# Four edits to a planned transformer kernel: a closing GpSimd addition, the norm's root in four tasks, a repriced exp, and filler chosen unit by unit

## The chip, the cores and the metric

The kernel runs on one core of one Trainium2 chip. The metric is the device time of one execution in microseconds (us), median over runs; lower is better. Engine names in the profile: PE (TensorE matmuls) and PEld (its weight loads), DVE (VectorE), ACT (ScalarE), POOL (GpSimd), SP (SyncE, which only issues transfers here).

## The reference, cut to what matters

Two layers share one set of weights. Each layer is an attention block with 32 heads of 16 features, then a dense block with a ReLU, each behind a layer norm and added to x. x has 2048 rows of 512 features; the dense block is 1792 wide.

```python
scores = jnp.einsum("bhqd,bhkd->bhqk", q, k) * (Dh ** -0.5)
p = _softmax(scores, axis=-1)
o = jnp.einsum("bhqk,bhkd->bhqd", p, v)
...
x = x + _A_ref(_layernorm(x, axis=-1), A_wqkv, A_wo)
x = x + _B_ref(_layernorm(x, axis=-1), B_w1, B_w2)
x = x + _A_ref(_layernorm(x, axis=-1), A_wqkv, A_wo)
x = x + _B_ref(_layernorm(x, axis=-1), B_w1, B_w2)
```

The softmax needs the exponential of 2 x 32 x 2048 x 2048 scores. The kernel cuts them into units of 128 keys by 512 queries of one head, 4096 units in all (later chunks with fewer queries put several blocks into a unit).

## The kernel before, in words

**Slots.** The main loop (`while units`) goes in slots. A slot takes three units: PE computes their scores into one of two PSUM tiles `ps_s` (L1714), and ACT takes the exponential of that tile into a buffer `e` in one instruction (L1727). There are 1366 slots.

**Integer pairs.** ACT need not do all units. In most slots the third unit is left out of ACT's instruction and goes to DVE, which adds a bias and makes a 16-bit integer `lin` out of it (L1299), whose bits read as bf16 are a coarse exponential. Two such units make a pair. GpSimd makes two shifted copies of a pair, `up` and `down`, with 64-bit integer additions (L1354), and PE sums values against all three versions, so that the errors cancel. A pair therefore saves ACT two units of 512 columns and costs DVE two instructions, GpSimd two, and PE three value products in place of one for each unit. Whether a slot starts a pair is decided from the plan's clocks: free buffers, the backlog of DVE (`now_dve[0] + waiting < now_pe[0] + BACKLOG`, 3000 ns), GpSimd's queue, and `press()`, the pressure of dated filler.

**Value rounds and filler.** Between the score matmuls PE does value products (L1175, into `ps_o`, four heads at once in a round) and filler: projections, the dense block, transposes (L564, L645, into `ps_f`). Every filler group ends in a DVE instruction that takes its sums out of PSUM (L745, L781, L835, L874, L914 and others).

**The plan.** All instructions are put in order on the host while the program is built, by a planner that keeps a clock for PE, DVE, GpSimd and SP and a price for each step: a matmul unit is `MM` = 216 ns, a DVE evacuation 612 ns, an exp `1280.0 * place[m] / (W * QS) + 63.3` ns (1280 for 1536 columns). `exp_end[no]` is when the plan expects slot `no`'s exp to end. From it comes `limit`, up to which PE may be filled before the next scores. `fill_pe(limit)` does filler while the account `owed` is above zero (each slot adds `pace`, what is left over what remains of the chunk). `fill_v(limit, least)` does value rounds, each with at least `least` of the four column groups ready (3 before). A slot calls them as filler, rounds, filler, or, when at least four slots' exps are pending, as rounds, filler, rounds. If PE then still has time in the plan, the scores are computed again up to that time (`times`), which keeps the PE clock up. DVE's tasks wait in `dve_q` and are taken by `run_dve` in order of rank and place; `musts`, the integer pairs' first steps and the copies of `ps_o`, go ahead of them. An engine runs its instructions in the order written, so the order of the plan is what the chip does, whenever operands are ready.

**The layer norm.** `ln_stats` (L600) per row block of 128, then `ln_root`: aggregation (L606), variance plus epsilon (L607), a seed of the reciprocal root by integer arithmetic (L611), a cubic step and a Newton step (L622 to L628), then `ln_apply` (L636), which makes `xn`; SP transposes `xn` by transfer, or PE does. The plan has the root as one task of `RSTD` = 1600 ns, put at the head of DVE's queue (`place=0`). There are 13 roots of four row blocks, 3 of two, 2 of one.

**The head.** Ahead of the loop the first norm is written out by hand: GpSimd builds the identity (masks.py:199, an affine-select), DVE reduces it to masks (L1387), takes statistics of the first four row blocks (L600), and GpSimd takes the root by a power (L1413). Then `xn` (L1425), transposes (L645), K and Q of the first heads (L1443), the first scores. ACT interleaves the first weight columns (`wkq`, L213), GpSimd the others, and loads two of the weight blocks itself (`load_w(nc.gpsimd, k, 1)`, L209). A trial INT64_ADD (L1474) follows. Constants such as `X_AT` and `WQ_AT` tell the plan when loads are there; the plan's clock starts with `exp_end = {-1: 11350.0, 0: 12350.0}`.

**The tail.** After the last scores, the last chunk's output projection, norm and dense block run on PE, DVE and ACT; GpSimd has nothing left.

Of the kernel before, what the change touches and what calls it, by code (L numbers as in the profile page):

```python
# [13 lines left out]
I32 = mybir.dt.int32  # L14
# [4 lines left out]
ALU = mybir.AluOpType  # L19

EPS = 1e-5
GAIN = 64.0 / 9.0
RSQRT_SEED = 0x5F3759DF
# [3 lines left out]
def kernel(  # L27
# [10 lines left out]
    nc = tc.nc  # L38
# [13 lines left out]
    QS = 512  # L52
# [5 lines left out]
    W = 3  # L58
# [33 lines left out]
    LOADED, FIRST_LOAD = 18000.0, 30  # L92
    BOTH = 4
    WHOLE = 4
    STARTS, MORE, LEAST, SLIP = {}, {}, {}, {}
    X_AT = (8.3, 8.5, 9.5, 10.6, 11.0, 11.4, 11.8, 12.1, 12.5, 12.8, 13.3, 14.0)
    WQ_AT, WV_AT = {0: 0.0, 1: 10600.0, 2: 16000.0, 3: 17400.0}, 10200.0
    FIRST_TRANSPOSE = 1600.0
    VLAG = 1
    RSTD = 1600.0  # L100
    Q_SPARE = 6
    V_LATE, CALM = 3, 1.2
    AHEAD = (8.0, 8.0)
# [77 lines left out]
    stats = [sb([P, TPC, nc.vector.BN_STATS_DIM], FP32, f"stats{n}") for n in range(2)]  # L181
    mv = [sb([P, TPC, nc.vector.BN_AGGR_DIM], FP32, f"mv{n}") for n in range(2)]
    va2 = sb([P, 2, TPC], FP32, "va")
    va_ = [va2[:, n] for n in range(2)]
    ya2 = sb([P, 2, TPC], FP32, "ya")
    ya_ = [ya2[:, n] for n in range(2)]
# [110 lines left out]
    two = [True]  # L297
# [98 lines left out]
    def do_piece():  # L396
        c, fn, ready, kind = cur.popleft()
        pe_run(kind, c, ready)
        fn()
        owed[0] -= c  # L400
# [9 lines left out]
            worst = max(worst, units_due / max(when - slot[0] - 1, 0.5))  # L410
        return worst

    def fill_pe(limit):

        while owed[0] > 0:
            limit_now = limit if owed[0] < 5.0 or not hurry[0] else now_pe[0] + 1000.0
            if not cur:
                if len(evac) > two[0]:
                    return
                free = bank_free[next_bank()] + DVE_TO_PE  # L420
                start = pe_start("f", free) + 50.0
                for g in urgent + sorted(work, key=lambda g: g.get("waits", False)):
                    t = at(g["deps"], "pe")
                    if t is not None and t <= start:
                        break
                else:
                    return
                if pe_start(g["kind"], free) + 50.0 + g["pieces"][0][0] * MM > limit_now:
                    return
                start_group(g)  # L430
            elif pe_start(cur[0][3], cur[0][2]) + cur[0][0] * MM > limit_now:
                return
            do_piece()

    def do_task(t):
        if t["engine"] == "pool":
            pool_q.remove(t)
            now_pool[0] = max(now_pool[0], at(t["deps"], "pool")) + t["cost"]
        else:
            dve_q.remove(t)  # L440
            dve_run(t["cost"], at(t["deps"], "dve"))
        t["fn"]()
        for k in t["makes"]:
            if k not in made:
                mark(k, t["engine"])
# [148 lines left out]
    def ln_n(tag):  # L594
        return ln_seq.index(tag) % 2
# [3 lines left out]
            ln_seq.append(tag)  # L599
        nc.vector.bn_stats(out=stats[ln_n(tag)][:, i, :], in_=x_t[tt][:])  # L600

    def ln_seed(tag, rows, gain):

        n = ln_n(tag)
        for i in range(rows):
            nc.vector.bn_aggr(out=mv[n][:, i, :], in_=stats[n][:, i, :])  # L606
        nc.vector.tensor_scalar(  # L607
            out=va_[n][:, 0:rows], in0=mv[n][:, 0:rows, 1], scalar1=EPS, scalar2=gain,
            op0=ALU.add, op1=ALU.mult,
        )  # L610
        nc.vector.tensor_scalar(  # L611
            out=ya_[n][:, 0:rows].bitcast(I32), in0=va_[n][:, 0:rows].bitcast(I32), scalar1=-0.5,
            scalar2=float(RSQRT_SEED), op0=ALU.mult, op1=ALU.add,
        )

    def ln_root(tag, rows):

        n = ln_n(tag)
        ln_seed(tag, rows, GAIN)
        a, y, t1 = va_[n][:, 0:rows], ya_[n][:, 0:rows], ta_[n][:, 0:rows]  # L620
        stt = nc.vector.scalar_tensor_tensor
        nc.vector.tensor_mul(out=t1, in0=y, in1=y)  # L622
        nc.vector.tensor_mul(out=t1, in0=t1, in1=a)
        stt(out=t1, in0=t1, scalar=-10.0 / 3.0, in1=t1, op0=ALU.add, op1=ALU.mult)
        stt(out=y, in0=t1, scalar=5.0, in1=y, op0=ALU.add, op1=ALU.mult)
        stt(out=t1, in0=y, scalar=-0.5 / GAIN, in1=y, op0=ALU.mult, op1=ALU.mult)
        nc.vector.tensor_mul(out=t1, in0=t1, in1=a)
        stt(out=y, in0=t1, scalar=1.5, in1=y, op0=ALU.add, op1=ALU.mult)  # L628

    xn_waits = [0]  # L630
    xn_free = [0.0]
# [27 lines left out]
    def ln_rows(tag, tt, n, i):  # L659

        if tag not in ln_seq:
            ln_seq.append(tag)
        at_tag = ln_seq.index(tag)
        prev = ln_seq[at_tag - 1]
        rows_of_prev = chunks[prev[1:]][1]
        before_that = ln_seq[at_tag - 2] if at_tag > 1 else None
        old = each(chunks[before_that[1:]][1], "xn", before_that) if at_tag > 1 else []
        if ("st", tag, i) not in made:
            loaded = [("x", tt + i)] * (tag[0] == "ln1" and not tag[1])
            task(720, lambda: ln_stats(tag, tt + i, i), [("st", tag, i)], old + loaded)  # L670
        if i == n - 1:

            task(
                RSTD, lambda: ln_root(tag, n), [("rs", tag, 3)], each(n, "st", tag) + old, place=0
            )

            def apply(k):
                ln_apply(tag, tt + k, k)
                if not by_dma(tag):
                    return  # L680
                _, l, j = tag
                xn_waits[0] -= k == TPC - 1
                nc.sync.dma_start_transpose(
                    out=xnT[j][:, :, k * P : (k + 1) * P], in_=xnbuf[k][:]
                )
                sp_free[0] = max(sp_free[0], now_dve[0] + 200.0) + first_transpose[0]
                first_transpose[0] = 0.0
# [50 lines left out]
    def each(n, *key):  # L738
        return [key + (i,) for i in range(n)]
# [237 lines left out]
    segs = []  # L977
# [38 lines left out]
    sums_wait = [0]  # L1016
# [150 lines left out]
    pend = deque()  # L1167
# [15 lines left out]
    seg_at = [0]  # L1183
# [55 lines left out]
            finish_segment(sg, sg is segs[-1])  # L1239
            seg_at[0] += 1  # L1240

    def fill_v(limit, least):

        done = 0
        while not sums_wait[0] and seg_at[0] < len(segs):
            if two[0] and (len(pend) < BOTH or cur or evac):
                break
            t = v_start()
            if t + MM > limit:
                break  # L1250
            sg = segs[seg_at[0]]
            found = v_ready(sg, t)
            if len({f[1][2] for f in found}) < min(least, sum(r > 0 for r in sg["rem"])):
                break
            v_round(found, t)
            done += 1
        return done
# [126 lines left out]
    tag = ("ln1", 0, 0)  # L1384
    idle_matmuls(13)
    for e in range(2):
        nc.vector.tensor_reduce(  # L1387
            out=mask[e],
# [4 lines left out]
            out=qmask[:, e : e + 1],  # L1393
# [5 lines left out]
            op0=ALU.mult,  # L1399
# [166 lines left out]
    while units:  # L1566
# [121 lines left out]
        need_by = exp_end[no - 1] - MM - PE_TO_ACT  # L1688
        limit = max(need_by - 60.0, s_ready) - SWITCH + SLIP.get(no, 0.0)
        late = len(pend) >= 4  # L1690
        for kind in ("v", "f", "v") if late else ("f", "v", "f"):
            if kind == "f":
                fill_pe(limit)
            else:
                fill_v(limit, LEAST.get(no, 3))

        spare = int(max(need_by - pe_start("s", s_ready), 0.0) / MM)
        soon = (len(pend) > 1) + (owed[0] > 1.0 and (bool(cur) or not evac and any(
# [33 lines left out]
            if a >= place[m]:  # L1732
                tc.declare_no_dep(ex.ins, score, reason="different PSUM banks")
        begin = max(exp_end[no - 1], now_pe[0] + PE_TO_ACT)
        exp_end[no] = begin + 1280.0 * place[m] / (W * QS) + 63.3
        for reader, banks in readers[no % 2]:
            if W - 1 in banks and len(banks) == 1:
                tc.declare_no_dep(
# [36 lines left out]
    while True:  # L1775
        t = next(
            (t for t in dve_q + pool_q if at(t["deps"], t["engine"]) is not None), None
        )
        if t is None:
            break  # L1780
        do_task(t)
    users.clear()
    l, j = 1, LAST
    tag = ("ln2", l, j)
# [169 lines left out]
```

## Time and profile before

| | us |
|---|---|
| Median of 3 runs | 1454.89 (1453.84 to 1458.4) |
| The profiled execution | 1457.04 |
| Its span, first to last instruction | 1455.3 |
| ACT busy | 1388.2 (95%) |
| PE busy | 1367.2 (94%) |
| DVE busy | 1137.0 (78%) |
| POOL busy | 711.3 (49%) |
| Mean granted PE clock | 0.987 |

The profile is of one execution. The busy time of an engine is the union of its instructions' times, so on ACT, where one exp starts before the last has drained, it hides short waits. "Idle before" counts gaps ahead of an instruction, and what is named behind it is what ended the wait; "issue" is a wait for nothing that the profile shows. The chain of waits goes back from the last instruction to whatever released each step. Some matmul records can be missing.

### The profile page before, as it was taken

How to read it: one execution, taken by the hardware profiler on the slowest of the kernel's cores; microseconds unless marked ns; L12 is line 12 of the kernel's file. 1: busy time of each engine (PE TensorE's matmuls, PEld its weight loads, DVE VectorE, ACT ScalarE, POOL GpSimd, SP SyncE). 2: the span in 40 equal slices, each digit the busy share in tenths (PEclk: the TensorE clock that was granted, in tenths of full speed). 3: DMA queues.
4: the chain of work that ended last, by engine and by line, in shares of the span. 5: the costliest groups of instructions: out<-in, count | busy, mean ns of one | idle time of the engine just before them, and what ended most of it. 6: DMA issues, size and time to landing. Idle time of an engine off the chain costs nothing.

```text
span 1455.3 us, 49098 instructions
## 1 busy us (share of the span) xinstructions
PE 1367.2 (94%) x20895; PEld 497.9 (34%) x20898; DVE 1137.0 (78%) x2078; ACT 1388.2 (95%) x1392; POOL 711.3 (49%) x1203
## 2 busy tenths in 40 slices
PE   6899889999999999999899999989999999999997
PEld 2322222222232222222222222223234444455665
DVE  5777668877887888887698777788888787877773
ACT  4999999999999999999999998999999999999994
POOL 3125555655545555565346453444544555555430
PEclk8999999999899999999999999999999999999999
DMA  5300000210102110121101100000110111132121
GB/s 131 96 5 17 21 21 2 46 39 17 24 8 47 28 31 10 29 49 25 23 2 31 34 5 2 6 18 17 42 42 16 43 37 25 30 83 66 26 49 31
DMA packets 135036, 46.41 MB, mean 32 GB/s; under 512 B 119680, under 2 KB 132032, under 8 KB 134816
## 3 DMA queue, kind: packets, MB, share of 16 engines
q1 hardware_dynamic: 127760, 37.14, 10.9%
q0 software_dynamic: 5568, 5.15, 1.9%
q8 instruction: 163, 2.67, 0.8%
q10 hardware_dynamic: 1488, 0.98, 0.2%
q14 instruction: 57, 0.47, 0.1%
HBM read 24.38 MB, written 2.10 MB: 18 GB/s over the span
## 4 chain that ended last, share of the span: by engine, by line
ACT 50%; PE 35%; DVE 12%; issue 3%; POOL 0%; DMA 0%; DVEq 0%; another core or an unknown queue 0%; ACTq 0%; POOLq 0%
ACT e L1727 50%; PE ps_s L1714 12%; PE ps_o L1175 11%; PE ps_f L564 10%; DVE lin L1299 5%; DVE stats L600 1%; PE ps_s L1801 1%; DVE vaug L781 1%; DVE ht L874 1%; PE ps_f L645 1%; DVE xn L636 0%; PE ps_f L557 0%; DVE ya L611 0%; DVE x L914 0%; DVE u L1060 0%
## 5 line engine op out<-in xcount | busy, mean ns | idle before, releaser
L1727 ACT ACTIVATE e<-ps_s 128x1024 bf16<-128x1024 f32 (+1 forms) x1366 | 1377.3, 1148 | 30.3 <-PE ps_s L1714 25.4
L1299 DVE TENSOR_SCALAR lin<-ps_s 128x512 int16<-128x512 f32 x1106 | 743.8, 686 | 179.8 <-PE ps_s L1714 124.9
L1354 POOL INT64_ADD up<-lin x553 | 340.0, 619 | 587.4 <-PE ps_o L1175 305.0
L1714 PE MATMUL ps_s<-q,ktp 32*128 32x512 bf16 (+2 forms) x5971 | 574.2, 328 | 45.2 <-ACT e L1727 27.6
L1354 POOL INT64_ADD down<-lin x553 | 342.2, 621 | 106.6 <-DVE lin L1299 50.4
L1175 PE MATMUL ps_o<-e,vaug 128*32 128x512 bf16 (+2 forms) x4124 | 365.2, 330 | 8.0 <-DVE r L1060 2.8
L1714 PEld LDWEIGHTS <-ktp 32*128 32x128 bf16 x5971 | 169.6, 91 | 513.5 <-issue 500.9
L1175 PEld LDWEIGHTS <-vaug 128*32 128x32 bf16 x7256 | 169.2, 95 | 228.7 <-issue 203.3
L1175 PE MATMUL ps_o<-up,vaug 128*32 128x512 bf16 (+2 forms) x1508 | 177.8, 324 | 0.0
L1175 PE MATMUL ps_o<-lin,vaug 128*32 128x512 bf16 (+2 forms) x1508 | 169.6, 324 | 1.6 <-DVE u L1060 1.0
L1175 PE MATMUL ps_o<-down,vscaled 128*32 128x512 bf16 (+2 forms) x1392 | 170.8, 326 | 0.0
L564 PE MATMUL ps_f<-xnT,w 128*32 128x512 bf16 (+1 forms) x1792 | 124.2, 356 | 4.6 <-DVE ht L874 2.1
L564 PE MATMUL ps_f<-w,ht 128*32 128x512 bf16 x1680 | 127.0, 382 | 1.3 <-DVE ht L874 0.5
L564 PE MATMUL ps_f<-xnT,wkq 128*32 128x512 bf16 (+2 forms) x1376 | 97.6, 357 | 3.9 <-DVE vaug L781 1.5
L874 DVE TENSOR_SCALAR ht<-ps_f 128x512 bf16<-128x512 f32 x105 | 71.7, 683 | 18.8 <-PE ps_f L564 16.9
L1175 PEld LDWEIGHTS <-vscaled 128*32 128x32 bf16 x1392 | 58.3, 96 | 20.6 <-issue 8.9
L564 PEld LDWEIGHTS <-w 128*32 128x32 bf16 x1792 | 38.8, 95 | 45.8 <-issue 36.8
L564 PEld LDWEIGHTS <-ht 128*32 128x32 bf16 x1680 | 34.7, 95 | 42.2 <-issue 29.1
L564 PEld LDWEIGHTS <-wkq 128*32 128x32 bf16 x1376 | 31.2, 96 | 39.2 <-issue 29.7
L600 DVE BATCH_NORM_STATS2 stats<-x 128x6 f32<-128x512 bf16 x63 | 42.4, 684 | 0.4
L564 PE MATMUL ps_f<-wv,xnT 128*32 128x512 bf16 x496 | 39.0, 383 | 3.8 <-DVE vaug L781 2.2
L564 PE MATMUL ps_f<-wo,ot 128*32 128x512 bf16 x496 | 38.4, 383 | 0.8 <-DVE x L835 0.5
(143 smaller groups left out, 537.4 us busy)
## 6 DMA issues: line engine op xcount, KB each, us to landing
w<-in_B_w_dram SPq DMA_DIRECT2D x144, 128.0 KB
q<-xn SPq DMA_DIRECT2D x44, 64.0 KB
out_dram<-x SPq DMA_DIRECT2D x15, 128.0 KB
x<-in_A_x_dram SPq DMA_DIRECT2D x14, 128.0 KB
ktp<-in_B_w_dram SPq DMA_DIRECT2D x10, 128.0 KB
r<-u POOLq DMA_DIRECT2D x8, 128.0 KB, 4.5
u<-u POOLq DMA_DIRECT2D x8, 128.0 KB, 4.6
u<-r POOLq DMA_DIRECT2D x6, 128.0 KB, 4.4
```

Source lines behind the costliest of these rows:

```text
L564: nc.tensor.matmul(out[cols], lhsT[:, cols], rhs, start=i % k == 0, stop=i % k == k - 1, tile_position=(0, 32 * g), skip_group_check=True,)
L600: nc.vector.bn_stats(out=stats[ln_n(tag)][:, i, :], in_=x_t[tt][:])
L645: ins = nc.tensor.transpose(pt[:, c * P : (c + 1) * P], xnbuf[i][:, c * P : (c + 1) * P], ident[:])
L781: nc.vector.tensor_copy(out=v_out(l, kb), in_=v_in(b))
L874: nc.vector.tensor_scalar(out=out, in0=sums, scalar1=0.0, scalar2=None, op0=ALU.max)
L1175: nc.tensor.matmul(ps_o[32 * g : 32 * g + 32, 0 : sg["w"]], values[:, 4 * sg["T"] + g, 2 * e : 2 * e + 32], rhs, start=g not in sg["begun" ...
L1299: first = nc.vector.tensor_scalar(out=lin[which][:, half * QS : (half + 1) * QS], in0=src, scalar1=EXP_BIAS, scalar2=THIRD, op0=ALU.add, o ...
L1354: nc.gpsimd.int64_add(words(out), words(line), by)
L1714: score = nc.tensor.matmul(b[:, a : a + sg["w"]], kt[32 * g : 32 * g + 32, kc : kc + P], qbuf[sg["n"] % 2][32 * g : 32 * g + 32, sg["e"], ...
L1727: ex = nc.scalar.activation(out=eb[:, 0 : place[m]], in_=b[:, 0 : place[m]], func=ACTF.Exp, scale=1.0 / (LOG2E * UNIT),)
L1801: uses(nc.tensor.matmul(out, lhsT, rhs, start=first, stop=last), b, needs=needs)
```

## The change

1. Behind the main loop and its last tasks, one standard GpSimd addition is put: `half_ya[0]` plus itself into `half_va[0]`, whose values nobody reads any more.
2. The root's instructions are the same, in the same order, but they are four DVE tasks (aggregate, seed, cubic, newton) priced at 155 ns per row block, 700, 780 and 580 ns, each waiting for the one before. They go to the end of DVE's queue and no longer to its head.
3. The plan's price of an exp has 50.0 instead of 63.3 ns beside the columns.
4. Once value rounds have begun (`two[0]` is false), a slot's free PE time is given out one step at a time. A step is the first of these that can be done: one filler unit that is owed; one value round with all four column groups; one value round with three; one filler unit ahead of what is owed, up to 8 units. With four or more slots pending the first two change places. `fill_pe` and `fill_v` get a `most` for that, and `fill_pe` a `floor`.

```diff
-    STARTS, MORE, LEAST, SLIP = {}, {}, {}, {}
+    STARTS, MORE, SLIP = {}, {}, {}
+    PRESSED, AHEAD_BY = 4, 8.0
...
-    RSTD = 1600.0
...
-    def fill_pe(limit):
-
-        while owed[0] > 0:
+    def fill_pe(limit, floor=0.0, most=99):
+
+        done = 0
+        while owed[0] > floor and done < most:
...
             do_piece()
+            done += 1
+        return done
...
+    def ln_steps(tag, rows):
...
+        def aggregate():
+            for i in range(rows):
+                nc.vector.bn_aggr(out=mv[n][:, i, :], in_=stats[n][:, i, :])
...
+        return aggregate, seed, cubic, newton
...
-            task(
-                RSTD, lambda: ln_root(tag, n), [("rs", tag, 3)], each(n, "st", tag) + old, place=0
-            )
+            made_last = each(n, "st", tag) + old
+            for k, step in enumerate(ln_steps(tag, n)):
+                task((155 * n, 700, 780, 580)[k], step, [("rs", tag, k)], made_last)
+                made_last = [("rs", tag, k)]
...
-    def fill_v(limit, least):
+    def fill_v(limit, least, most=99):
...
-        while not sums_wait[0] and seg_at[0] < len(segs):
+        while done < most and not sums_wait[0] and seg_at[0] < len(segs):
...
         late = len(pend) >= 4
-        for kind in ("v", "f", "v") if late else ("f", "v", "f"):
-            if kind == "f":
-                fill_pe(limit)
-            else:
-                fill_v(limit, LEAST.get(no, 3))
+        if two[0]:
+            for kind in ("v", "f", "v") if late else ("f", "v", "f"):
+                if kind == "f":
+                    fill_pe(limit)
+                else:
+                    fill_v(limit, 3)
+        else:
+            while True:
+                late = len(pend) >= PRESSED
+                steps = [lambda: fill_pe(limit, most=1), lambda: fill_v(limit, 4, 1)]
+                steps = (steps[::-1] if late else steps) + [
+                    lambda: fill_v(limit, 3, 1), lambda: fill_pe(limit, -AHEAD_BY, 1)
+                ]
+                if not any(step() for step in steps):
+                    break
...
-        exp_end[no] = begin + 1280.0 * place[m] / (W * QS) + 63.3
+        exp_end[no] = begin + 1280.0 * place[m] / (W * QS) + 50.0
...
         do_task(t)
+    nc.gpsimd.tensor_add(out=half_va[0][:], in0=half_ya[0][:], in1=half_ya[0][:])
     users.clear()
```

More of the change, by code (lines that the diff above doesn't have):

```diff
@@ L418, in fill_pe @@
                 if len(evac) > two[0]:
-                    return
+                    return done
                 free = bank_free[next_bank()] + DVE_TO_PE
@@ L426, in fill_pe @@
                 else:
-                    return
+                    return done
                 if pe_start(g["kind"], free) + 50.0 + g["pieces"][0][0] * MM > limit_now:
-                    return
+                    return done
                 start_group(g)
             elif pe_start(cur[0][3], cur[0][2]) + cur[0][0] * MM > limit_now:
-                return
+                return done
             do_piece()
+            done += 1
+        return done
     def do_task(t):
@@ L600, in ln_stats, with ln_root @@
         nc.vector.bn_stats(out=stats[ln_n(tag)][:, i, :], in_=x_t[tt][:])
-    def ln_seed(tag, rows, gain):
+    def ln_root(tag, rows):
+        for step in ln_steps(tag, rows):
+            step()
+    def ln_steps(tag, rows):
         n = ln_n(tag)
[L605 to L609, printed above, removed]
-        )
[L611 to L614, printed above, removed]
@@ L616, in ln_root @@
-    def ln_root(tag, rows):
-        n = ln_n(tag)
-        ln_seed(tag, rows, GAIN)
         a, y, t1 = va_[n][:, 0:rows], ya_[n][:, 0:rows], ta_[n][:, 0:rows]
         stt = nc.vector.scalar_tensor_tensor
[L622 to L628, printed above, removed]
+        def aggregate():
+            for i in range(rows):
+                nc.vector.bn_aggr(out=mv[n][:, i, :], in_=stats[n][:, i, :])
@@ new lines, in seed, with cubic @@
+        def seed():
+            nc.vector.tensor_scalar(
+                out=a, in0=mv[n][:, 0:rows, 1], scalar1=EPS, scalar2=GAIN, op0=ALU.add,
+                op1=ALU.mult,
+            )
+            nc.vector.tensor_scalar(
+                out=y.bitcast(I32), in0=a.bitcast(I32), scalar1=-0.5, scalar2=float(RSQRT_SEED),
+                op0=ALU.mult, op1=ALU.add,
+            )
+        def cubic():
+            nc.vector.tensor_mul(out=t1, in0=y, in1=y)
+            nc.vector.tensor_mul(out=t1, in0=t1, in1=a)
+            stt(out=t1, in0=t1, scalar=-10.0 / 3.0, in1=t1, op0=ALU.add, op1=ALU.mult)
+            stt(out=y, in0=t1, scalar=5.0, in1=y, op0=ALU.add, op1=ALU.mult)
@@ L630, with newton @@
+        def newton():
+            stt(out=t1, in0=y, scalar=-0.5 / GAIN, in1=y, op0=ALU.mult, op1=ALU.mult)
+            nc.vector.tensor_mul(out=t1, in0=t1, in1=a)
+            stt(out=y, in0=t1, scalar=1.5, in1=y, op0=ALU.add, op1=ALU.mult)
+        return aggregate, seed, cubic, newton
     xn_waits = [0]
@@ L671, in ln_rows @@
         if i == n - 1:
-            task(
-                RSTD, lambda: ln_root(tag, n), [("rs", tag, 3)], each(n, "st", tag) + old, place=0
-            )
+            made_last = each(n, "st", tag) + old
+            for k, step in enumerate(ln_steps(tag, n)):
+                task((155 * n, 700, 780, 580)[k], step, [("rs", tag, k)], made_last)
+                made_last = [("rs", tag, k)]
             def apply(k):
```

## The prediction

> **What bounds the kernel now.** I read the page first, then the groups of instructions by shape, then the start (chain of waits, waits, windows), then the middle. One measured execution is the base: 1457.04 us with a span of 1455.3 us, so 1.7 us lie around the span; it stands 2.15 us above the median of the three runs (1454.89).
>
> From the page, the engines' busy time:
>
> ```profile
> PE 1367.2 (94%) x20895; PEld 497.9 (34%) x20898; DVE 1137.0 (78%) x2078; ACT 1388.2 (95%) x1392; POOL 711.3 (49%) x1203
> ```
>
> PE and ACT are both close to full, so a saving on one alone soon meets the other. What ACT does are the exps (groups by shape; count, busy us, mean ns, then idle before):
>
> ```profile
> L1727 ACT ACTIVATE e<-ps_s 128x1024 bf16<-128x1024 f32 x1106 | 1040.8, 1067 | 22.7 <-PE ps_s L1714 20.0 <-PE ps_o L1175 0.7 <-ACT e L1727 0.2
> L1727 ACT ACTIVATE e<-ps_s 128x1536 bf16<-128x1536 f32 x259 | 366.1, 1496 | 7.6 <-PE ps_s L1714 5.4 <-PE ps_o L1175 1.4
> ```
>
> The means overstate the price, because an exp begins while the one before drains. What an exp costs a full ACT is the distance between starts. The timeline has one stretch of 1024-column exps, the chain of waits one of 1536, and two pairs of windows find where each stretch's next exp starts (the count goes up by one):
>
> ```profile
> 543.98 10.19 ACT L1727 ACTIVATE e<-ps_s 128x1024 bf16<-128x1024 f32 x11
> 543.97:553.91 9.94, 9.94 (x12) 1.00 0.05 10
> 543.97:553.93 9.96, 9.96 (x13) 1.00 0.05 10
> ```
>
> ```profile
> 38.16 22.58 ACT e L1727 x18
> 39.49:51.46 11.97, 11.97 (x10) 1.00 0.46 73
> 39.49:51.48 11.99, 11.99 (x11) 1.00 0.46 73
> ```
>
> One exp before 543.98 still runs in the window, so the twelfth of the stretch starts at 553.92: 9.94 us / 11 = 0.904 us. Likewise (51.47 - 38.16) / 10 = 1.331 us. So ACT at its fastest needs 1106 x 0.904 + 260 x 1.331 = 1346 us for 1366 exps. They run from 22.35 to 1429.8 us (timeline) = 1407 us. **61 us** are lost among the exps, 22 us lie ahead of them, 25 us behind.
>
> The 22 us ahead: the chain of waits, the waits and the windows (busy of PE, PEld, DVE, ACT, POOL; then granted clock, DMA share, GB/s).
>
> ```profile
> 0.83 0.18 POOL ident masks.py:197
> 1.07 8.44 issue
> 9.52 0.29 POOL ident masks.py:199
> 9.83 0.22 DVE masks L1387
> 10.81 1.19 DVE stats L600 x2
> ```
>
> ```profile
> POOL ident masks.py:199 <- issue: 8.5, 1, 8.5
> POOL up L1474 <- issue: 5.9, 1, 5.9
> ```
>
> ```profile
> 6.70:14.70 8.00, 0.00 (x0) 0.00 (x0) 4.73 (x18) 1.29 (x2) 5.06 (x22) 0.69 1.01 296
> 14.70:18.00 3.30, 3.21 (x19) 2.11 (x20) 1.09 (x5) 1.07 (x2) 2.46 (x10) 0.50 1.15 186
> ```
>
> GpSimd stands for 8.44 us before its first affine-select and for 5.9 us before its first INT64_ADD, waiting for no other engine. The trace's records hold two pool-configuration instructions at 1.03 and 1.06 us and two at 21.59 and 21.63 us, and nowhere else: its code is changed there, to the standard set at the start and to the 64-bit set for the exps' integer part. Between those points standard operations (L1413, 0.77 us) run without such a wait, and so do 1106 INT64_ADDs. The first change is needed because the execution before ended on INT64_ADDs. Behind it VectorE waits (mask reductions before the statistics, in order), and PE idles 8 us, after which its clock is 0.50.
>
> **Part 1, the closing addition: -9.0 us.** It leaves the standard set loaded, so that the next execution starts with it. If the load of a set that is there already takes nothing: affine-select at 1.1 instead of 9.52; mask reductions end at 2.5; the statistics wait for x0 and x1, whose landing records say 3.47 and 3.65, so 3.5 instead of 10.72 (7.2 earlier). xn begins at 6.9 (was 14.12), the transposes at 7.5; ACT's xnT copies start at 8.1, when wkq's interleave (6.63 + 1.37) frees ACT, instead of 15.44. The second transposes follow xn at 8.9 (were 17.33, held back by four idle matmuls of 0.43 us at half clock). PE has then idled 0.8 us, not 8, so I take the clock as full: K and Q (19.46 to 21.1 now) begin at 10.3, behind the DVE copies, and end at 11.3; the first exp starts near 12.6 instead of 22.35, 9.7 us earlier. Taken off: 0.7 us, since GpSimd's two 128 KB weight loads (now at 10.66 us) move to 2.2 us, onto DMA engines that deliver some 300 GB/s: 256 KB / 300 GB/s = 0.85 us, most of it on wkq. Bounds: -7.2 (DVE's shift alone) to -9.9; 0 if the load is paid anyway. By the landing records the x rows of later chunks are all there by 10.7 us and still come before their statistics. The plan's own constants speak for such a start: exp 0 ends there at 12.35 us and wkq[1] is ready at 10.6, while the trace has 23.8 and 17.8.
> The addition itself (0.74 us, like L1413) and its load (8.44) stand behind the last INT64_ADD, at 1421.6 us; the tail of PE, DVE and ACT goes on to 1454 us, 33 us of cover. Nothing else is queued on GpSimd there. Cost: nothing; without the cover 9.2 us.
>
> **Part 2, exps at 50 instead of 63.3 ns overhead: -5 us.** 1280 x 1024 / 1536 + 50 = 903.3 and 1280 + 50 = 1330 are the measured 904 and 1331. Before, the plan gave PE 13.3 ns too much work per slot; where PE sets the pace, ACT waits for that. At most 1366 x 13.3 ns = 18.2 us. PE carries about 35% of the chain that ended last: 0.35 x 18.2 = 6.4; I take 5. Bounds: -18.2, and +8 if the trimmed plan starts fewer integer pairs (rivals).
>
> **Part 3, the root in four tasks: -1 us.** The instructions are the same; from the rows, four aggregations 4 x 154 + 335 + 427 + 250 + 217 + 5 x 162 = 2655 ns, near the new price 2680, where 1600 was planned. Other DVE work may now come in between, the integer pairs' first step above all. What waited for that, of PE's waits in 60 to 1421 us:
>
> ```profile
> PE ps_s L1714 <- DVE lin L1299: 11.8, 12, 1.6
> ```
>
> Not all of the twelve stand behind a root. The root also loses its place at the head of the queue, so xn comes later; behind it wait the transposes (SP's queue, or PE) and K, Q and V of a later chunk, due some slots on. Bounds: -11.8 to +4 (18 roots by some 0.2 us of semaphores or a late K).
>
> **Part 4, filler and value rounds one at a time, filler up to 8 units ahead: -3 us.** What it can use is the PE time that the plan fills with repeated scores:
>
> ```profile
> L1714 PE MATMUL ps_s<-q,ktp 32*128 32x512 bf16 x3375 | 434.1, 388 | 42.5 <-ACT e L1727 26.9 <-DVE lin L1299 10.4 <-DVE ktp L745 0.9
> ...
> L1714 PE MATMUL ps_s<-q,ktp 32*128 32x256 bf16 x1548 | 106.3, 272 | 2.0 <-DVE lin L1299 1.4 <-ACT e L1727 0.4
> ...
> L1714 PE MATMUL ps_s<-q,ktp 32*128 32x128 bf16 x1048 | 38.4, 216 | 0.8 <-issue 0.5 <-ACT e L1727 0.3
> ```
>
> In units of 512 columns these are 3375 + 1548/2 + 1048/4 = 4411; the reference needs 2 x 32 x 16 x 4 = 4096. So 315 units, 105 rounds of the plan's 216 ns = 22.7 us, are repeats. Filler moved into them no longer crowds a later slot, but it pays only where that slot made ACT wait, and those repeats were put in to keep PE's clock. Of the 21.6 us that exps visibly waited for scores (60 to 1421 us) I take an eighth. Bounds: -22.7 to +10.
>
> **Sum.** -9.0 - 5 - 1 - 3 = -18.0: 1457.0 becomes 1439.0, and less the 2.15 us to the median, **1437 us**. A measurement here tells 0.3% from nothing, 4.4 us: faster is below 1450.5, slower above 1459.3.
>
> **Rivals.**
> *The first load is paid whatever is resident.* The program issues it without knowing what ran before. For: the 8.44 us differ from the second load's 5.7, so the time is not of one kind only. Against: the constants above. Time: 1437 + 9 = 1446; range 1440 to 1456. 12%.
> The Trainium skill's GPSIMD Engine Reference, Instruction dispatch, has the first call after a pool-configuration instruction pay about 6 us (measured there 5.95) and names no exception for a set already loaded; by that page this rival would hold. The second load here, 5.7 us, agrees with it; the first is longer, and no run yet has the standard set loaded twice in a row.
> *The plan's edits gain nothing*, since PE's work is the same and what leaves one slot crowds another: PE is busy 1296.6 of the 1361 us in 60 to 1421. Time: 1454.9 - 9 = 1446. 12%.
> *Slower: fewer integer pairs.* Each pair takes 2 x (1.331 - 0.904) = 0.854 us off ACT. A pair is refused while the plan's DVE clock and its waiting tasks are 3.0 us ahead of PE's. The honest root price puts 13 x 1.08 + 3 x 0.77 + 2 x 0.62 = 17.6 us more on that clock; at 2 x 0.612 us of DVE for a pair, 14 pairs. The plan's exps shrink by 18.2 us, at 1.9 us a pair another 9. 23 pairs cost 19.6 us; it decides from 21 pairs on (18 / 0.854) if the other gains stay, from 11 if only the start gains. With no plan gain: 1446 + 20 = 1466. Against: DVE is 78% busy and POOL 49%, and only the first of the four tasks is counted as waiting. 16%.
> The rest, 2%, is a better plan than I think, below 1418.
>
> **How the numbers follow.** The forecast has 58% (own range 1424 to 1448). Of the paid load's 12%, 8 lie below 1450.5 and 4 within 0.3%; of the plan that gains nothing 10 and 2; of the fewer pairs 14 above 1459.3 and 2 within (so 16 in all); the far gain has 2. Faster 0.58 + 0.08 + 0.10 + 0.02 = 0.78, same 0.04 + 0.02 + 0.02 = 0.08, slower 0.14. The range 1418 to 1457 leaves out the slower cases and the far gain, 0.16.
>
> **What would show it.** Right: affine-select near 1.1 us, no issue wait of 8 us there, statistics at 3.5, first exp at 12 to 13, PE's clock 1.0 in 7 to 20 us, a pool load at 1421 to 1430 us with the end unmoved; about 553 pairs; exps' loss 45 to 58 us instead of 61; fewer repeated scores. Wrong: the 8.4 us wait still there; under 540 pairs; more exps of 1536 columns; a longer loss between 200 and 1400 us.

## The result, and the profile after

The changed kernel takes 1448.41 us (median of 10 runs, 1446.06 to 1454.44) against 1456.33 for before (10 runs): ratio 0.9957, 95% interval 0.9941 to 0.9973, that is 6 us less by the means (8 by the medians). 18 were forecast (1437), with a range of 1418 to 1457. One of the ten runs of before was slow (1511.79 us) and is not in the ratio. The profiled execution takes 1452.35 us with a span of 1450.6, 4.7 less than the profiled one of before.

The start first: the chain of waits and the waits of 0 to 60 us (us in total, times, longest), then the same two windows as before (busy of PE, PEld, DVE, ACT, POOL; clock, DMA share, GB/s).

```profile
0.73 2.55 DMA x<-in_A_x_dram
...
3.30 1.29 DVE stats L603 x2
```

```profile
POOL up L1488 <- issue: 5.7, 1, 5.7
```

```profile
6.70:14.70 8.00, 7.34 (x87) 3.97 (x87) 5.84 (x14) 4.49 (x7) 3.93 (x17) 1.00 0.94 275
14.70:18.00 3.30, 3.07 (x45) 0.99 (x46) 2.85 (x10) 3.29 (x4) 2.24 (x4) 1.00 0.73 163
```

The 8.44 us of "issue" (time in which GpSimd waited for nothing that the profile shows) ahead of the affine-select are gone; the chain now starts with the landing of x. The second load, ahead of the first INT64_ADD, is there as before. PE works where it idled, at full clock. Timeline: affine-select at 1.30, first exp at 12.14 us.

```profile
1.30 0.29 POOL masks.py:199 TENSOR_SCALAR_AFFINE_SELECT ident<-ident 128x128 bf16<-128x128 bf16 x1 [0.29 <-POOL ident masks.py:197]
12.14 4.27 ACT L1751 ACTIVATE e<-ps_s 128x1536 bf16<-128x1536 f32 x3 [0.19 <-PE ps_s L1738]
...
1434.29 0.18 POOL L1806 TENSOR_TENSOR half_va<-half_ya 128x2 f32<-128x2 f32 x1 [6.90 <-issue]
```

The last row is the closing addition, behind a load of 6.90 us; the program ends at 1450.6, so it is covered.

So the start gained 10.2 us, more than the wait itself: from the first transposes to the first exp it took 5.15 us instead of 7.55, with PE's clock at 1.00 instead of 0.50. The rest of the span, by its busy times (page) and the groups by shape:

```profile
PE 1367.0 (94%) x20874; PEld 501.1 (35%) x20876; DVE 1108.0 (76%) x2025; ACT 1407.3 (97%) x1392; POOL 673.6 (46%) x1144
```

```profile
L1751 ACT ACTIVATE e<-ps_s 128x1024 bf16<-128x1024 f32 x1046 | 990.1, 1127 | 16.6 <-PE ps_s L1738 9.8 <-PE ps_o L1189 5.6
L1751 ACT ACTIVATE e<-ps_s 128x1536 bf16<-128x1536 f32 x319 | 454.6, 1540 | 3.6 <-PE ps_o L1189 2.4 <-PE ps_s L1738 0.8
L1738 PE MATMUL ps_s<-q,ktp 32*128 32x512 bf16 x3381 | 434.5, 386 | 40.5 <-ACT e L1751 33.0 <-DVE lin L1313 3.3 <-DVE q L1495 0.3
L1738 PE MATMUL ps_s<-q,ktp 32*128 32x256 bf16 x1596 | 108.2, 272 | 3.2 <-ACT e L1751 2.4 <-DVE lin L1313 0.2
L1738 PE MATMUL ps_s<-q,ktp 32*128 32x128 bf16 x1144 | 41.9, 217 | 2.1 <-ACT e L1751 1.6 <-issue 0.2 <-DVE lin L1313 0.2
```

ACT is busier, PE the same, DVE and POOL less busy. Exps of 1024 columns went from 1106 to 1046, and those of 1536 from 259 to 319: 60 units of 30 pairs went back to ACT. The repeated scores grew too: 3381 + 1596/2 + 1144/4 = 4465 units, 123 rounds instead of 105. What PE's scores still wait for DVE's first step is down (waits, 60 to 1421 us):

```profile
PE ps_s L1738 <- DVE lin L1313: 3.7, 10, 1.3
```

A span splits into four terms: the time of the first exp; what the exps need at the prediction's 0.904 and 1.331 us; what is lost among them; and the tail behind the last exp. Need and loss together are the stretch from the first exp to the end of the last. The loss is what is left of the span when the other three are taken off, so that the terms always add up. For the profiled execution of every kernel of this study (first and last exp from the timeline, exps' shapes and pairs from the groups):

| kernel | ratio to before (95%) | pairs | first | need | loss | tail |
|---|---|---|---|---|---|---|
| before | 1 | 553 | 22.3 | 1345.9 | 61.5 | 25.5 |
| the change | 0.9957 (0.9941 to 0.9973) | 523 | 12.1 | 1371.5 | 45.6 | 21.3 |
| e1 addition only | 0.9931 (0.9912 to 0.9949) | 553 | 12.3 | 1345.9 | 59.3 | 26.0 |
| e2 no addition | 1.0015 (1.0003 to 1.0027) | 523 | 21.6 | 1371.5 | 39.0 | 21.3 |
| e5 addition, price | 1.0017 (1.0003 to 1.0032) | 553 | 12.3 | 1345.9 | 56.4 | 39.4 |
| e9 addition, root | 1.0011 (0.9998 to 1.0024) | 554 | 12.2 | 1345.0 | 58.3 | 42.7 |
| e6 addition, choice | 1.0016 (1.0000 to 1.0032) | 542 | 12.3 | 1355.3 | 75.2 | 18.8 |
| e3 addition, price, root | 0.9921 (0.9907 to 0.9935) | 554 | 12.2 | 1345.0 | 47.5 | 39.1 |
| e10 addition, price, choice | 0.9939 (0.9919 to 0.9960) | 533 | 12.2 | 1363.0 | 45.3 | 21.4 |
| e11 addition, root, choice | 0.9892 (0.9876 to 0.9908) | 538 | 12.4 | 1358.7 | 48.4 | 20.0 |
| e4 change, rounds first from 3 | 1.0061 (1.0046 to 1.0076) | 557 | 12.1 | 1342.5 | 50.0 | 59.5 |
| e7 as e3, less PE work | 0.9736 (0.9720 to 0.9752) | 564 | 12.5 | 1336.5 | 39.1 | 26.5 |
| e8 as e3, no repeats | 1.0036 (1.0023 to 1.0049) | 552 | 12.5 | 1346.7 | 54.9 | 43.5 |
| e12 change, exp at 56 | 0.9864 (0.9845 to 0.9883) | 539 | 12.2 | 1357.8 | 45.1 | 21.6 |
| e13 as e6, more repeats | 1.0055 (1.0036 to 1.0074) | 535 | 12.3 | 1361.3 | 66.7 | 18.9 |
| e14 as e12, more repeats | 0.9905 (0.9886 to 0.9923) | 536 | 12.4 | 1360.4 | 45.5 | 21.3 |

The change itself: start -10.2, need +25.6, loss -15.9, tail -4.2, together -4.7 us.

The four terms are of one execution each, the ratios of 4 to 12 runs of a kernel. The profiled execution took 1452.35 us of the changed kernel (median 1448.41), 1463.33 of e6 (1457.54), 1443.71 of e10 (1449.43), 1455.19 of e2 (1458.76); the others lie within 3 us of their medians. By so much a loss in the table can be off.

### The profile page after: what moved, and what is told of

Same layout as the page of the kernel before. It is cut to its first block, busy times and chain, and to the rows that moved or that the text cites. A ratio compares the mean times of both kernels' runs of the same rounds, so it can differ in the third digit from the quotient of the medians.

```text
span 1450.6 us, 48895 instructions
## 1 busy us (share of the span) xinstructions
PE 1367.0 (94%) x20874; PEld 501.1 (35%) x20876; DVE 1108.0 (76%) x2025; ACT 1407.3 (97%) x1392; POOL 673.6 (46%) x1144
## 3 DMA queue, kind: packets, MB, share of 16 engines
q0 software_dynamic: 5568, 5.15, 1.9%
## 4 chain that ended last, share of the span: by engine, by line
ACT 65%; PE 26%; DVE 7%; issue 2%; DMA 0%; DVEq 0%; ACTq 0%
ACT e L1751 65%; PE ps_s L1738 9%; PE ps_o L1189 8%; PE ps_f L567 7%; DVE lin L1313 3%; PE ps_s L1826 1%; DVE ht L888 1%; PE ps_f L560 0%; DVE stats L603 0%; PE ps_f L658 0%; DVE ktp L759 0%; DVE xn L830 0%; DVE u L1074 0%; DVE vaug L795 0%; DVE ta L638 0%
## 5 line engine op out<-in xcount | busy, mean ns | idle before, releaser
L1751 ACT ACTIVATE e<-ps_s 128x1024 bf16<-128x1024 f32 (+1 forms) x1366 | 1396.4, 1223 | 21.0 <-PE ps_s L1738 11.3
L1313 DVE TENSOR_SCALAR lin<-ps_s 128x512 int16<-128x512 f32 x1046 | 704.0, 686 | 191.8 <-PE ps_s L1738 157.9
L1368 POOL INT64_ADD up<-lin x523 | 321.2, 620 | 617.2 <-PE ps_o L1189 387.4
L1368 POOL INT64_ADD down<-lin x523 | 321.0, 618 | 108.7 <-PE ps_o L1189 48.7
L1738 PEld LDWEIGHTS <-ktp 32*128 32x128 bf16 x6121 | 181.7, 92 | 524.8 <-issue 510.6
L1189 PEld LDWEIGHTS <-vaug 128*32 128x32 bf16 x7192 | 174.8, 95 | 240.9 <-issue 211.7
L1189 PE MATMUL ps_o<-down,vscaled 128*32 128x512 bf16 (+2 forms) x1284 | 161.1, 327 | 0.0
L567 PE MATMUL ps_f<-w,ht 128*32 128x512 bf16 x1680 | 138.7, 382 | 0.9 <-DVE x L928 0.5
L1189 PEld LDWEIGHTS <-vscaled 128*32 128x32 bf16 x1284 | 53.5, 96 | 27.2 <-issue 17.4
L567 PEld LDWEIGHTS <-wkq 128*32 128x32 bf16 x1376 | 31.7, 96 | 33.5 <-issue 25.6
```

Of the source, the lines that this page charges most:

```text
L567: nc.tensor.matmul(out[cols], lhsT[:, cols], rhs, start=i % k == 0, stop=i % k == k - 1, tile_position=(0, 32 * g), skip_group_check=True,)
L1189: nc.tensor.matmul(ps_o[32 * g : 32 * g + 32, 0 : sg["w"]], values[:, 4 * sg["T"] + g, 2 * e : 2 * e + 32], rhs, start=g not in sg["begun" ...
L1313: first = nc.vector.tensor_scalar(out=lin[which][:, half * QS : (half + 1) * QS], in0=src, scalar1=EXP_BIAS, scalar2=THIRD, op0=ALU.add, o ...
L1368: nc.gpsimd.int64_add(words(out), words(line), by)
L1738: score = nc.tensor.matmul(b[:, a : a + sg["w"]], kt[32 * g : 32 * g + 32, kc : kc + P], qbuf[sg["n"] % 2][32 * g : 32 * g + 32, sg["e"], ...
L1751: ex = nc.scalar.activation(out=eb[:, 0 : place[m]], in_=b[:, 0 : place[m]], func=ACTF.Exp, scale=1.0 / (LOG2E * UNIT),)
```

## The experiments

**The addition by itself, and everything but the addition.**

```diff
(e1: the kernel before)
         do_task(t)
+    nc.gpsimd.tensor_add(out=half_va[0][:], in0=half_ya[0][:], in1=half_ya[0][:])
(e2: the changed kernel, without that line)
```

> The kernel before with the closing addition and nothing else. Theory (the load at the start is spared and the whole shift reaches the end): affine-select at 1.3 us, first exp at 12.1 instead of 22.3 us, still 553 pairs and the exps' stretch still 1407 us, so the time is 10 us below before: about 1446. Rival (the shift is eaten by DVE's work or loads behind the head): first exp at 12.1 but a stretch longer by 3 us or more, about 1449 to 1452.

> The changed kernel without the closing addition. Theory: the 8.4 us wait before the first affine-select is back, first exp at 22.3 us, 523 pairs as in the changed kernel, time 10 us above the changed kernel: about 1458, that is no better than before, so that the three edits of the plan together bring nothing. Rival (the addition also costs something at the end, or the plan's edits need the earlier start): under 1455 or over 1461.

e1: 1445.33 us against 1456.19, a ratio of 0.9931 (-10 us), first exp at 12.3, stretch 1405, tail 26.0: the shift of the start reaches the end whole. e2: 1458.76 us, the wait back, first exp at 21.6, ratio 1.0015. So the addition is the whole gain, and the plan's three edits together cost 2 us (0.4 to 4) where a gain of 9 was forecast. Beside the addition they cost 3 (1448.41 against 1445.33). Neither rival came.

**The old choice, and an earlier turn to value rounds.** The first theory was that the 30 lost pairs were the missing gain.

```diff
(e3: the changed kernel with the old loop)
+        for kind in ("v", "f", "v") if late else ("f", "v", "f"):
...
-            while True:
(e4: the changed kernel)
-    PRESSED, AHEAD_BY = 4, 8.0
+    PRESSED, AHEAD_BY = 3, 8.0
```

> The changed kernel with the old choice of filler and value rounds (filler, rounds, filler, or rounds first where four slots are pending), keeping the addition, the four root tasks and the exp at 50 ns. Theory (the one-at-a-time choice holds back the pairs' value products, so that buffers stay taken and 30 pairs are not started, which is 26 us of exps): 554 pairs, exps' loss between the 46 us of the changed kernel and the 61 us of before, time 1433 to 1441. Rival (PE is the bound, so that pairs won back are lost again as waits for scores): 554 pairs, exps' loss 65 to 72 us, time 1446 to 1449.

> The changed kernel with value rounds ahead of filler from three pending slots on, not from four. Theory (the pairs' products wait behind filler): 557 pairs, GpSimd's waits for PE's reads of its buffers back from 387 us to about 300 us, exps' loss 46 to 55 us, time 1424 to 1434. Rival (PE is the bound): 557 pairs and an exps' loss of 65 to 75 us, time 1444 to 1449. Second rival (filler comes too late when rounds go first): long waits for scores or keys at the ends of chunks, time over 1449.

Both have their pairs back, and both end their exps at 1404.6 or 1404.7 us, 25 us before the changed kernel. But e3 takes 1445.31 us, no better than the addition alone, and e4 1465.88, slower than before. The theory fell, and so did its rival as stated, for the loss is low (47.5 and 50.0). What grew is the tail. The windows behind the last exp of e1, e3, e4 and the changed kernel:

```profile
1417.50:1443.50 26.00, 19.78 (x271) 14.31 (x259) 8.55 (x28) 6.35 (x19) 0.00 (x0) 0.93 0.05 16
```

```profile
1404.70:1443.80 39.10, 29.60 (x394) 20.57 (x379) 9.42 (x30) 10.63 (x26) 0.18 (x1) 0.98 0.27 65
```

```profile
1404.60:1464.10 59.50, 44.54 (x679) 28.90 (x671) 9.83 (x29) 14.79 (x32) 0.00 (x0) 0.97 0.32 77
```

```profile
1429.30:1450.60 21.30, 16.23 (x261) 12.73 (x260) 9.10 (x31) 6.22 (x18) 0.18 (x1) 1.00 0.07 20
```

PE has 16.2 us of work behind the last exp of the changed kernel, nearly all of it the last chunk's own; 19.8 in e1, 29.6 in e3, 44.5 in e4. What is above 16 is mostly filler that found no room beside the exps: in the window of e4 stand 224 matmuls of the dense block's second product (13.4 us), of which the changed kernel has none there. What PE could not do in time waits for the end, where ACT has only 6 to 15 us of work.

The second rival of e4 had this in part: filler does come too late, and the time is over 1449. But it comes behind the last exp and not as waits at the ends of chunks (PE's score matmuls of 512 columns stood idle for 39.8 us in all, 40.5 in the changed kernel). For e3 neither theory had it. The pairs alone do not make the tail: e1 has 553 of them and a tail of 26.0.

GpSimd's copies tell of the pairs' fate (us in total, times, longest, in the changed kernel and in e4; before: 305.0):

```profile
POOL up L1368 <- PE ps_o L1189: 387.4, 145, 11.2
```

```profile
POOL up L1368 <- PE ps_o L1189: 310.3, 137, 6.7
```

With filler unit by unit, GpSimd waits longer for PE to be done with its buffers; with rounds first from three pending slots it does not, and the pairs return. That much of the first theory holds. Which of the plan's conditions refuses the pairs was not looked at.

**Is PE the bound?**

```diff
(e7: the kernel of e3)
-            [(ht[ft][:, a : a + P], w2[:, ft, :]) for ft in range(NF)], fin,
+            [(ht[ft][:, a : a + P], w2[:, ft, :]) for ft in range(0, NF, 2)], fin,
(e8: the kernel of e3)
-        times = 1 + min(spare, max(0, math.ceil(short / MM)))
+        times = 1
```

> The kernel of the old choice (addition, root in four tasks, exp at 50 ns; 1445.3 us), which here leaves out every other term of the dense block's second product in all groups but the last chunk's: 7 of 14 units for each row block, 31 groups, some 47 us of PE work, and nothing of ACT's. 564 pairs, exps at their fastest 1336 us. Theory (PE's work is the bound): the filler left behind the last exp shrinks, tail 39 to about 26 us, loss 38 to 44 us, time 1410 to 1422, at least 23 us less. Rival (ACT is the bound, and PE's work only fills its gaps): 9 us less for the ten pairs, about 1436.

> The kernel of the old choice without its 105 rounds of repeated scores (552 pairs, 23 us less PE work, nothing of the result left out). Theory (the repeats lie in time that PE could not use otherwise): time 1444 to 1450, clock at or under 1.0, loss the same 46 to 52 us, tail 38 to 42. Rival A (the repeats take PE time that filler could have had): 1430 to 1438. Rival B (they keep the clock up): granted clock under 0.97 and time over 1455.

e7, which leaves out half the terms of the dense block's second product: 1417.7 us, 28 less than e3, for 47 us less PE work by the plan's prices (PE busy 1321.2 us instead of 1359.0) and ten pairs more: the theory's time. 12.6 us came from the tail, 8.5 from the pairs, 8.4 from the loss. ACT as the bound would have given 9.

e8: 1461.72 us, 16 more than e3, for less work. The theory was wrong, and so was rival A; of rival B the time is right and the size of the cause is not: the granted clock is 0.984 to 0.986 in its runs, not under 0.97, where e3 has 0.998 to 1.0. 1.4% of PE's busy 1359 us is an estimated 19 us. PE is busy as long as in e3 (1359.4 and 1359.0 us), though it has 105 rounds less to do. So the repeats pay for themselves, and the lower clock is large enough to be the reason; the plan changed a little too (two pairs fewer).

**The plan's edits one by one,** each with the addition.

```diff
(e5: the kernel before with the addition)
-        exp_end[no] = begin + 1280.0 * place[m] / (W * QS) + 63.3
+        exp_end[no] = begin + 1280.0 * place[m] / (W * QS) + 50.0
(e6: the one-at-a-time choice alone; e9: the root in four tasks alone)
(e10: the changed kernel)
-            for k, step in enumerate(ln_steps(tag, n)):
+            task(
+                1600.0, lambda: ln_root(tag, n), [("rs", tag, 3)], each(n, "st", tag) + old, place=0
+            )
(e11: the changed kernel with 63.3 for 50.0)
```

> The kernel before with the closing addition and the exp at 50 ns; root and choice as before. 553 pairs, so the exps need 1345 us at their fastest. Theory (PE's work is the bound: what the shorter slots no longer hold stays over for the time behind the last exp): exps' loss down from 60 us (addition alone) to 46 to 50, stretch about 1393 us, tail up from 26 to 36 to 40 us, time 1443 to 1447, the same as the addition alone (1445.3). Rival (the price helps by itself, the tail of the old choice came from the root's four tasks): loss 46 to 50, tail 26 to 28, time 1432 to 1436.

> The kernel before with the closing addition and the one-at-a-time choice; exp at 63.3 ns, root in one task of 1600. 542 pairs, exps at their fastest 1355 us. Theory (the choice does filler earlier, which shortens the tail, and holds back the pairs' products, which costs pairs; the two cancel): tail 21 us, loss 50 to 56 us, time 1440 to 1446. Rival (most of the 30 pairs were lost through the choice alone): time 1447 to 1450, as the changed kernel.

> The kernel before with the closing addition and the root in four tasks; exp at 63.3 ns, choice as before. 554 pairs, exps at their fastest 1344 us. Theory (the root as one task kept the integer pairs' first steps waiting; with four tasks PE's waits for them fall from 11.8 to about 1.5 us, and the filler that is left over goes behind the last exp): exps' loss 46 to 54 us instead of 60, tail 38 to 42 instead of 26, time 1444 to 1449, as the addition alone (1445.3). Rival (the root's split is a gain of its own): same loss, tail 26 to 29, time 1432 to 1437.

> The changed kernel with the root back in one task of 1600 ns. 533 pairs, exps at their fastest 1362 us. Theory (it is the root that takes the waits away): PE's waits for the pairs' first steps 9 to 13 us, exps' loss 54 to 64 us, tail 21, time 1451 to 1460, slower than the changed kernel (1448.4) though it has ten pairs more. Rival (time follows the pairs): loss 46, time 1440 to 1444.

> The changed kernel with the exp back at 63.3 ns. 538 pairs, exps at their fastest 1358 us, filler nearly done at the last exp. Theory (15 pairs lost are enough to clear the filler, the changed kernel loses 30): loss 46 to 53 us, tail 20 to 22, time 1439 to 1446. Rival (the right price of the exp is what lowers the loss): loss 58 to 64 us, time 1450 to 1456.

Each edit alone loses all that the addition gains: 1458.31 (price), 1458.02 (root) and 1457.54 us (choice) against 1445.3 for the addition alone. Price and root: tails of 39.4 and 42.7 us, about as the theories said, but the loss hardly fell (56.4 and 58.3), so the times of 1443 to 1449 were missed. The choice: its tail is short (18.8), its loss 75.2 instead of 50 to 56 (some 69 at its median time, if the difference lies in the loss), and theory and rival both missed the time. Two edits at a time are better: price and root 1445.31; price and choice 1449.43, between the theory's time and the rival's; root and choice 1440.87, in which the theory was right throughout (loss 48.4, tail 20.0). So the edits do not add up. Beside the choice, the exp's price of 50 ns costs 7.5 us where the root is in four tasks (1448.41 against 1440.87) and gains 8 where it is one (1449.43 against 1457.54). The waits of PE for the pairs' first step, in e1 and e9 (60 to 1400 us), follow the root's four tasks:

```profile
PE ps_s L1714 <- DVE lin L1299: 11.8, 12, 1.6
```

```profile
PE ps_s L1728 <- DVE lin L1313: 1.1, 4, 0.4
```

e10, with the root in one task, has 7.8 us of them, and still a loss of 45.3 in its profiled execution, the fastest of six. Its median is 5.7 us longer, which puts the loss at some 51 at most, still under the 54 to 64 of the theory that these waits make it. With two or three of the edits the loss is 39 to 48 us, with one 56 to 75.

Loss and tail together tell more than either. In the kernels that have the choice of the change with the price, the root or both they are 60 to 68 us (e2, e10, e11 and the changed kernel; e12 and e14 below too). In all others that do the whole work, e4 among them, they are 85 to 110. In the first group more pairs go with shorter times, if not strictly: 1440.87 us with 538 (e11), 1449.43 with 533 (e10), 1448.41 with 523 (the change).

**Towards a faster version.**

```diff
(e12: the changed kernel)
-        exp_end[no] = begin + 1280.0 * place[m] / (W * QS) + 50.0
+        exp_end[no] = begin + 1280.0 * place[m] / (W * QS) + 56.0
(e13: the kernel of e6; e14: the kernel of e12)
-    STREAMED, WINDOW = 0.56, 3413.0
+    STREAMED, WINDOW = 0.60, 3413.0
```

> The changed kernel with the exp at 56 ns instead of 50. 539 pairs, exps at their fastest 1357 us, 14 filler units left at the last exp as in the changed kernel. Theory (PE and ACT end together with about 15 pairs fewer, not 30): loss 44 to 50 us, tail 20 to 22, time 1436 to 1442, faster than the addition alone. Rival (pairs cost PE what they save ACT, so that the sixteen pairs more come back as loss): loss 58 to 62 us, time 1447 to 1451.

> The kernel of the choice alone (1457.5 us at a granted clock of 0.981 to 0.989, exps' loss 76 us), with more repeated scores: the plan keeps PE streaming 0.60 of its 3413 ns window, not 0.56. 535 pairs, 181 rounds of repeats instead of 123, filler nearly done at the last exp as before. Theory (PE is the bound, and the throttled clock took its time): clock 0.996 or more, loss 46 to 56 us, time 1442 to 1448 in spite of 58 rounds (12.5 us) more PE work and seven pairs fewer. Rival (the order of the plan makes the waits): clock up, loss still over 65 us, time 1457 to 1470.

> The changed kernel with the exp at 56 ns (1437.2 us, clock 0.993 to 0.999) and PE kept streaming 0.60 of the window. 536 pairs, 171 rounds of repeats instead of 113. Theory (the clock is nearly full already, so the repeats only cost): 1437 to 1442. Rival (the last thousandths of the clock are worth more): under 1435.

e12 takes 1437.24 us, ratio 0.9864: 19 us under before, 11 under the changed kernel, and faster than the addition alone. Loss and tail are those of the changed kernel; it starts 16 pairs more, which is 13.7 us of exps, and PE still ends as early (window behind its last exp; 16.6 us of PE):

```profile
1415.20:1436.80 21.60, 16.61 (x247) 12.81 (x246) 9.16 (x31) 6.23 (x18) 0.18 (x1) 1.00 0.06 20
```

e13: 1462.96 us. The clock rose from 0.981 to 0.993 between the profiled executions, the loss only fell from 75.2 to 66.7, in the rival's range: the clock is a smaller part. That the order of the plan is the larger one, as the rival has it, is left over, not shown. e14: 1441.37 us at a clock of 0.999 to 1.0, as the theory had it: more repeats only cost here.

## Why the prediction was wrong

**The step that failed.** The sum took the pairs as unchanged (about 553) and added -5, -1 and -3 for the plan's edits as if each kept its gain beside the others. The runs show 523 pairs, which is 25.6 us more of exps, against 20.1 us less of loss and tail; in the two profiled executions that leaves 5.5 us on the wrong side, and by all runs the three edits cost 2 us (e2) where 9 were to be gained.

**The bound.** The two exp prices, 0.904 and 1.331 us, held: the median distance from the start of one exp to the next is 0.904 or 0.905 us behind 1024 columns and 1.330 to 1.334 behind 1536 in the traces of all sixteen kernels. That PE is 94% busy beside ACT's 95% was read rightly, and then not used in the sum.

**Part 1, -9.0: right, by its steps.** Affine-select 1.30 (forecast 1.1), statistics 3.30 (3.5), xn 6.52 (6.9), transposes 6.99 (7.5), first exp 12.14 (12.6), full clock. e1 has -10 us by the ratio. The 0.7 us taken off for GpSimd's earlier weight loads were not needed: ACT's interleave starts at 5.46 us, where it was 6.63. The closing load ran to 1434.3, not 1430, because the last INT64_ADD came later, at 1426.8; the cover held.

**The rival that the load is paid anyway: refuted.** In the trace after, the two pool-configuration records stand at 1.21 and 1.24 us, and the affine-select runs at 1.30. Between the second of them and the affine-select lie 0.07 us. The Trainium skill's GPSIMD Engine Reference, Instruction dispatch, gives some 6 us for the first call to freshly loaded code. By the traces here the 64-bit set's 5.7 us agree with it, and the standard set's 6.9 and 8.44 are longer. The Trainium skill's section does not say what a set that is there already costs; that the rival follows from it was the prediction's own reading.

**Part 2 (price), -5; part 3 (root), -1; part 4 (choice), -3.** A smaller loss was there, and more of it than forecast: 16 us, where 9 had been taken for all three. What the sum left out is what pays for it. Part 2 said that PE gets 13.3 ns less work in each slot and did not ask where that work goes. With the old choice, price or root or both have tails of 39 to 43 us instead of 26. For the price that fits the work that left the slots; for the root, which takes no work out of them, the reason is not shown. Part 4's filler ahead goes with a short tail (21) and with fewer pairs: the choice by itself loses 11, beside the root 16, beside the price 20, beside both 31. That it displaces the value rounds by it is argued from GpSimd's waits and from e4, where earlier rounds bring 557 pairs. The -3 for part 4 was taken from the waits for scores; the number of pairs was no term of that part.

**The rivals.** "The plan's edits gain nothing, since PE's work is the same" gave 1446 and 12%. Its time is nearest (1448.4, and +2 us in e2), and e7 shows that PE's work counts. Its reason does not hold as stated: e12 edits the plan alone, PE is busy 1360.1 us in it against 1362.7 in e1, and it is 8 us faster than e1. The three edits gain nothing because two larger terms nearly cancel, and that the time comes out near the rival's is in part luck. "Fewer pairs" named 23 and there are 30, but not through DVE's planned clock alone, and its 1.9 us a pair stands in no row: price and root together (e3) keep 554. Beside the choice the price costs 9 or 15 pairs and the root 4 or 10. They cost less than 19.6 us net because loss and tail fell at the same time. Fewer pairs also take value products from PE (8338 of its matmuls by the groups, 8532 before); how much of that fall is due to them, no run separates.

**What would show it.** Of the signs named, under 540 pairs and more exps of 1536 columns are there. Of the signs that it is right, the loss is in the range named (45.6 us), and fewer repeated scores was wrong (123 rounds, where before has 105).

**Open.** Why one edit alone loses 12 to 13 us and two together lose 4 at most is not settled. The terms say where (tail for price and root, loss for the choice), e13 that the clock is not the main part of the choice's loss, e10 that PE's waits for the integer step do not account for the loss by themselves.

## What to carry to other kernels

When two engines are both above 90%, write the sum with a term for each: work taken out of one engine's way has to be done somewhere, and a place to look is behind the last instruction of the other engine. Where several edits share one planner, do not add their gains; here each of three lost 12 us or more beside the addition, and two of them together took up to 17 us less than one. In such a kernel a planner's price is also a dial that deals work between the two engines: the measured price of an exp (50) was the worst of the three tried in the changed kernel, 1448.4 us against 1437.2 with 56 and 1440.9 with 63.3. A start-up wait that depends on what the program left loaded can be moved behind the end, and was worth its full length here, where the start is one chain.

## What the runs showed of the hardware

The waits that stand behind GpSimd's pool-configuration records, read here as loads of its code: 8.44 us for the standard set in the start of the kernel before, 5.7 for the 64-bit set, 6.9 for the standard set at the end of the changed kernel; 0.07 us for the set that the execution before had left loaded. With and without the closing addition (e1, e2) the wait at the start goes and comes back.

Granted clock and time of one and the same kernel go together: the changed kernel's ten runs go from 1446.06 us at 1.0 to 1454.44 at 0.992, 8 us for 0.8%; 0.8% of PE's busy 1367 us would be 11 (an estimate). Taking out 105 rounds of repeated matmuls, some 23 us by the plan's price and read by nobody, made e8 16 us slower, at a clock of 0.984 to 0.986 instead of 0.998 to 1.0.
